# The last product of a short convolution: stepping on the output instead of on the inputs

## The chip, the cores and the metric

The kernel runs on one core of one Trainium2 chip. The metric is the device time of one execution in microseconds; the times given are medians over several runs. A profile is one execution taken by the hardware profiler, and its span runs from the first to the last instruction of the core.

## The reference

The inputs are bf16. A layernorm of `A_q` over its 640 channels feeds two branches, and the output is `x + A + B`, of shape 1x2048x640:

```
xn = layernorm(A_q)                                  # 2048 positions x 640 channels
# branch A: a short convolution (4 taps), a product with v, a long convolution over the sequence
k_shift[t] = sum over m of k[t - m] * shift_k[:, m]  # m = 0..3
kv   = k_shift * v
y    = irfft(rfft(kv padded to 4096) * rfft(ssm_k padded to 4096))[:2048] + kv * ssm_D
A    = xn * y
# branch B: a gated unit
B    = (sigmoid(xn @ w_gate) * (xn @ w_up)) @ w_down # 640 -> 1728 -> 640
out  = A_q + A + B
```

## The kernel before

Both branches run interleaved on the same engines. TensorE (PE) does the matmuls of branch B (gate and up on line 770, down on line 786) and also the transforms of the long convolution, written as small matmuls in four stages (st1 line 508, st2 line 528, st3 lines 580 and 582, st4 line 612). VectorE (DVE) and ScalarE (ACT) share the rest: results leave PSUM through `ev` (lines 314, 315 and 317), sigmoids are on ACT (lines 724, 729 and 735), the gated products on DVE (lines 726, 732 and 737), and the additions of the down product to `acc` on DVE (line 798).

The order of all this work is fixed. Each step is recorded as an operation with its reads and writes, and the lists `ORDER` and `ON_DVE` give the order of emission and the engine of the steps that could go to either. The durations that are passed to `dve(...)` or `pe(...)` don't change what is emitted. Each engine executes its own queue in that order. The matmuls of gate and up write two PSUM buffers `g`; the convolution uses three buffers `c`.

The 640 channels of the convolution are split into two halves of 4 groups of 80 channels; the partitions hold the 4 groups times 32 blocks of the sequence (n1), and the 64 positions in a block (n2) lie along the free dimension. A half is worked in 5 sub-blocks of 16 channels, 2 (`b`) times 8 (`j`), so there are 10 sub-blocks (`idx` 0 to 9). For each one `rec_kv` computes the taps and the product with v on DVE, all over 64 x 2 x 8 = 1024 elements per partition:

- line 470 multiplies a shifted slice of `kt` with a tap into `ta` or `tb`, line 471 does so for the third tap into the tile `kvt`, and line 475 adds the parts into `ta`;
- line 488, the last, multiplies `ta` with the slice of `vt` and writes `kvt`.

The tile `ta` has the layout [n, b, j] with j innermost. The slice of `vt` takes 8 neighbouring channels j, then the second 8 at 40 channels' distance, and the next position n at 80 channels' distance. The result must lie in `kvt` as [j, b, n] with n innermost, since st1 (line 508) loads, for each j, 128 neighbouring elements (b, n) of `kvt` as its stationary operand. `by_j` (line 451) gives this view of the tile. `PRM["KT"]` holds all ten indices, so the branch `kt` is taken each time.

So one instruction on line 488 also changes the layout: in the kernel before it is walked in the order of its output, (j, b, n), which is one run of 1024 elements, and reads `ta` in steps of 16 elements and `vt` in steps of 80.

Other lines that the text names: line 448 adds the diagonal `Dt` to every 64th element of a tile of the long filter `ht`; line 548 copies halves of the spectra `S` between partitions by DMA, and lines 552 to 567 form the products of the spectra on DVE; line 401 copies a table; lines 620 and 621 apply the result of the convolution to `acc`. Weights `w` of branch B come by DMA on SP's queue (lines 368 to 378).

Of the kernel before, what the change touches and what calls it, by code (L numbers as in the profile page):

```python
# [16 lines left out]
ALU = mybir.AluOpType  # L17
# [202 lines left out]
def kernel(  # L220
# [14 lines left out]
    nc = tc.nc  # L235
# [54 lines left out]
    tl = plan.tiles  # L290
# [18 lines left out]
    def dve(n, rate, fn, **kw):  # L309
        plan.op({"DVE": ((1.042 * n / rate + 70) * 1e-3, fn)}, **kw)  # L310
# [140 lines left out]
    def by_j(t):  # L451
        return t.rearrange("p b n j -> p (b n j)").rearrange("p (j b n) -> p j b n", j=JS, b=2)

    def rec_kv(idx, pri):
        half, sub = divmod(idx, NSUB)
        kb, vb = f"kt{half}", f"vt{half}"
        j0 = sub * JS
        a, o = f"ka{idx}", f"kvt{idx}"
        kr = [(kb, "h")] + [(kb, g) for g in range(G)]
        vr_ = [(vb, g) for g in range(G)]  # L460

        def sl(t, r0):
            return t[:, r0:r0 + N2, :].rearrange("p n (b j) -> p n b j", b=2)[:, :, :, j0:j0 + JS]

        def sh(m):
            s = sT[:, m:m + 1, half * HALF:(half + 1) * HALF].rearrange("p o (b j) -> p o b j", b=2)
            return s[:, :, :, j0:j0 + JS].to_broadcast((P, N2, 2, JS))

        def mul(c, m, al):
            dve(1024, 2, lambda: nc.vector.tensor_tensor(tl[c][:], sl(tl[kb], 3 - m), sh(m), ALU.mult) if c != o else  # L470
                nc.vector.tensor_tensor(tl[c].rearrange("p b n j -> p n b j"), sl(tl[kb], 3 - m), sh(m), ALU.mult),
                r=(kr if m else kr[1:]) + [("s",)], w=[(c,)], alloc=[(c, al)] if al else (), pri=pri)

        def add(c):
            dve(1024, 2, lambda: nc.vector.tensor_tensor(tl[a][:], tl[a][:], tl[c][:] if c != o else  # L475
                                                         tl[c].rearrange("p b n j -> p n b j"), ALU.add),
                r=[(c,)], w=[(a,)], pri=pri)
        t1, t2 = f"kb{idx}_1", f"kb{idx}_2"
        mul(a, 0, "ta")
        mul(t1, 1, "tb")  # L480
        mul(o, 2, "kvt")
        add(t1)
        mul(t2, 3, "tb")
        add(o)
        add(t2)
        kt = idx in PRM["KT"]
        form = "p n b j -> p j b n" if kt else "p n b j -> p b n j"
        dve(1024, 1 if kt else 2, lambda: nc.vector.tensor_tensor(by_j(tl[o]) if kt else tl[o][:], tl[a].rearrange(form),  # L488
                                                                  sl(tl[vb], 0).rearrange(form), ALU.mult),
            r=[(a,)] + vr_, w=[(o,)], pri=pri)  # L490

    def rec_st1(idx, x, pri, first):
# [364 lines left out]
    def conv():  # L857
        for s in range(-1, NI):
            nx = s + 1
            if nx < NI:  # L860
                rec_st1(nx, 1, ct(nx - 1) if nx else -1.0, True)
            if nx == 0:
                rec_kv(0, 8.0)
            if nx + 1 < NI:
                if nx + 1 == NSUB:
                    load_kv(1, ct(nx) - 10, nb=ct(nx) - PRM["KV1"])
                    load_h(1, 0, ct(nx) - 10, nb=ct(nx) - 20)
                if nx + 1 == NSUB + 2:
                    load_h(1, 1, ct(nx) - 10, nb=ct(nx) - 20)
                rec_kv(nx + 1, ct(nx))  # L870
            if nx < NI:
                rec_st1(nx, 0, ct(nx - 0.4), False)
            if s >= 0:
                rec_st2(s, ct(s))
                rec_prod(s, ct(s + 0.3))
                rec_st3(s, ct(s + 0.5))
                if s == NSUB - 1:
                    rec_st4(0, ct(s + PRM["ST4"]), False)
        rec_st4(1, ct(NI - 0.2), False)
# [48 lines left out]
```

## Time and profile before

| what | value |
|---|---|
| median of 3 runs | 260.01 us (258.31 to 262.99) |
| profiled execution, its own time | 262.01 us |
| its span | 259.9 us |
| granted TensorE clock, mean over the span | 0.978 |
| busy: PE, DVE, ACT | 244.0, 201.2, 175.5 us |
| line 488 on DVE | 10 instructions, 2131 to 2155 ns, first at 64.3 us, last at 194.4 us |
| line 508 on PE reading kvt | 320 matmuls, first at 67.6 us, last at 203.8 us |

The profile names an instruction by its line, its engine, its operation, and the tiles written and read (`out<-in`). Of a group it gives the shape, the number, the busy time in us, the mean of one in ns, and behind the second bar the engine's idle time just before these instructions with what ended most of it. A wait line reads "who waited <- for whom: us in total, times, longest". "Issue" is time in which an engine waited for nothing that the profile shows.

### The profile page before, as it was taken

The page shows a single profiled execution, that of the slowest core. Times are in us where ns is not written, and L with a number is a line of the kernel's source. Part 1 is how long each engine was busy: PE and PEld are TensorE (multiplying, and loading weights), DVE is VectorE, ACT ScalarE, POOL GpSimd, SP SyncE. Part 2 cuts the span into 40 slices and gives each one's busy share as a digit, 9 for nine tenths or more (in the row PEclk, how much of TensorE's full clock was granted, in tenths as well). Part 3 has the DMA queues.
Part 4 walks back from the last instruction along what each step waited for, and adds up shares of the span by engine and source line. Part 5 has one row for each costly group of instructions (what it writes and reads, how often), then busy time and mean ns, then how long its engine had stood idle before and what let it go on. Part 6 is the DMA issues. An engine that isn't in the chain of part 4 may idle for free.

```text
span 259.9 us, 9463 instructions
## 1 busy us (share of the span) xinstructions
PE 244.0 (94%) x4231; PEld 146.1 (56%) x4231; DVE 201.2 (77%) x337; ACT 175.5 (68%) x259; POOL 0.7 (0%) x6
## 2 busy tenths in 40 slices
PE   8999979999999999999999997899999999998980
PEld 2854436764445467666554554577676554556750
DVE  4623524768999899999999999579999998895630
ACT  3623779767888899788998885663899785441100
POOL 1000000000000000000000000000000000000000
PEclk9999999999999999999999999599999999999996
DMA  6999999999995528999999739934126476002823
GB/s 175 310 277 207 205 314 130 152 139 188 229 248 128 143 75 235 150 140 128 157 182 283 192 66 318 188 101 117 23 62 177 99 236 184 1 5 55 188 73 95
DMA packets 91024, 41.44 MB, mean 159 GB/s; under 512 B 66656, under 2 KB 88104, under 8 KB 90664
## 3 DMA queue, kind: packets, MB, share of 16 engines
q1 hardware_dynamic: 90600, 40.44, 73.6%
q8 instruction: 33, 0.54, 0.9%
q10 hardware_dynamic: 384, 0.41, 0.5%
q14 instruction: 7, 0.06, 0.1%
HBM read 30.61 MB, written 5.24 MB: 138 GB/s over the span
## 4 chain that ended last, share of the span: by engine, by line
PE 64%; DMA 18%; DVE 5%; SPq 4%; issue 3%; ACT 3%; DVEq 0%; ACTq 0%
PE g L786 25%; PE g L770 25%; DMA acc<-in_A_q_dram 9%; PE c L528 6%; DMA w<-in_B_w_up_dram 5%; DMA vt<-in_A_v_dram 3%; PE c L612 3%; PE c L580 3%; PE c L508 2%; DMA P<-S 2%; ACT S L314 1%; SPq L378 1%; SPq L352 1%; DVE hT L737 1%; SPq L827 1%
## 5 line engine op out<-in xcount | busy, mean ns | idle before, releaser
L770 PE MATMUL g<-xnT,w 128*128 128x512 bf16 x380 | 90.9, 379 | 2.6 <-ACT sig L735 1.3
L786 PE MATMUL g<-wd,hT 128*128 128x320 bf16 x448 | 68.5, 306 | 2.0 <-issue 2.0
L770 PEld LDWEIGHTS <-w 128*128 128x128 bf16 x380 | 34.7, 98 | 41.1 <-issue 2.6
L786 PEld LDWEIGHTS <-hT 128*128 128x128 bf16 x448 | 42.6, 99 | 19.4 <-issue 2.3
L314 ACT CAST S<-c 128x1024 bf16<-128x1024 f32 x40 | 39.4, 1026 | 8.1 <-PE c L528 8.0
L737 DVE TENSOR_TENSOR hT<-sig,g 128x512 bf16<-128x512 bf16 x32 | 21.9, 686 | 18.6 <-PE g L770 18.3
L770 PE MATMUL g<-xnT,V 128*128 128x512 bf16 x140 | 32.8, 379 | 0.0
L735 ACT ACTIVATE sig<-g 128x512 bf16<-128x512 f32 x32 | 19.2, 601 | 15.1 <-PE g L770 13.5
L798 DVE TENSOR_TENSOR acc<-g,acc 128x320 bf16<-128x320 f32 x32 | 15.5, 488 | 17.4 <-PE g L786 17.2
L528 PEld LDWEIGHTS <-Mt 64*128 64x128 f16 x1280 | 20.2, 96 | 8.7 <-issue 8.1
L528 PE MATMUL c<-T,Mt 64*128 64x64 bf16 x1280 | 22.8, 191 | 2.2 <-issue 2.2
L317 ACT ACTIVATE T<-c 128x1024 bf16<-128x1024 f32 x20 | 19.9, 1029 | 5.5 <-PE c L508 5.4
L770 PEld LDWEIGHTS <-V 128*128 128x128 bf16 x140 | 13.3, 98 | 15.7 <-DMA V<-in_B_w_up_dram 0.5
L488 DVE TENSOR_TENSOR kvt<-ta,vt 128x1024 bf16<-128x1024 bf16 x10 | 21.4, 2143 | 0.1
L314 ACT CAST V<-c 128x1024 bf16<-128x1024 f32 x18 | 18.2, 1026 | 3.2 <-PE c L580 3.1
L314 ACT CAST T<-c 128x1024 bf16<-128x1024 f32 x19 | 18.8, 1024 | 1.6 <-PE c L508 1.4
L729 ACT ACTIVATE sig<-g 128x512 bf16<-128x512 f32 x18 | 10.8, 602 | 5.0 <-PE g L770 3.3
L561 DVE TENSOR_TENSOR S<-S 128x1024 bf16<-128x1024 bf16 x20 | 13.8, 688 | 0.3
L475 DVE TENSOR_TENSOR ta<-ta,tb 128x1024 bf16<-128x1024 bf16 x20 | 13.8, 688 | 0.3
L470 DVE TENSOR_TENSOR tb<-kt,sT 128x1024 bf16<-128x1024 bf16 x20 | 13.8, 690 | 0.1
L567 DVE TENSOR_TENSOR S<-P 64x1024 bf16<-64x1024 bf16 x18 | 12.4, 689 | 0.6
L565 DVE TENSOR_TENSOR S<-S 64x1024 bf16<-64x1024 bf16 x18 | 12.4, 687 | 0.6
(82 smaller groups left out, 240.9 us busy)
## 6 DMA issues: line engine op xcount, KB each, us to landing
w<-in_B_w_gate_dram SPq DMA_DIRECT2D x7, 640.0 KB, 6.9
w<-in_B_w_up_dram SPq DMA_DIRECT2D x7, 640.0 KB, 5.2
P<-S SPq DMA_DIRECT2D x14, 256.0 KB, 3.7
kt<-in_A_k_dram SPq DMA_DIRECT2D x8, 320.0 KB, 6.3
vt<-in_A_v_dram SPq DMA_DIRECT2D x8, 320.0 KB, 7.1
xnd<-xq SPq DMA_DIRECT2D x4, 640.0 KB, 5.0
ht<-in_A_ssm_k_dram SPq DMA_DIRECT2D x16, 96.0 KB, 5.8
wd<-in_B_w_down_dram SPq DMA_DIRECT2D x3, 480.0 KB, 9.8
```

The lines of the kernel that those rows point to most:

```text
L314: fa = lambda: nc.scalar.copy(out=out_fn(), in_=in_fn())
L317: fa = lambda: nc.scalar.activation(out_fn(), in_fn(), ACT.Copy, scale=scale)
L470: dve(1024, 2, lambda: nc.vector.tensor_tensor(tl[c][:], sl(tl[kb], 3 - m), sh(m), ALU.mult) if c != o else nc.vector.tensor_tensor(tl[c]. ...
L475: dve(1024, 2, lambda: nc.vector.tensor_tensor(tl[a][:], tl[a][:], tl[c][:] if c != o else tl[c].rearrange("p b n j -> p n b j"), ALU.add) ...
L488: dve(1024, 1 if kt else 2, lambda: nc.vector.tensor_tensor(by_j(tl[o]) if kt else tl[o][:], tl[a].rearrange(form), sl(tl[vb], 0).rearrang ...
L528: nc.tensor.matmul(tl[c][:, b, 64 * kk:64 * kk + 64], lhsT=Mb[rows, k, 64 - 64 * r:192 - 64 * r], rhs=tl[T][rows, 2 * k + r].rearrange("p ...
L561: dve(n, 2, lambda b=b: nc.vector.tensor_tensor(X(b), X(b), H(b), ALU.mult), r=[(Z, b, 0)] + sr, w=[(S_, "p", b)], pri=pri + 0.01)
L735: act(512, lambda: nc.scalar.activation(tl[sg][:], pv(0), ACT.Sigmoid), r=[pk(0)], w=[(sg,)], alloc=[(sg, "sig")], pri=pri - 2000)
L737: dve(512, 1, lambda: nc.vector.tensor_tensor(hT[:, fc, :], tl[sg][:], pv(1), ALU.mult), r=[pk(1), (sg,)], w=[(hk, fc)], pri=pri - 2000)
L770: nc.tensor.matmul(tl[c][:], lhsT=w()[:, k, o:o + P], rhs=tl[X][:, k, :], start=(k == 0), stop=(k == NC - 1))
L786: nc.tensor.matmul(tl[pd[i]][:, 0:320], lhsT=hT[:, fc, t4 * P:(t4 + 1) * P], rhs=wd[:, fc, 320 * i:320 * i + 320], start=(fc == 0), stop=( ...
L798: dve(320, 1, lambda i=i, m=m, pd=pd: nc.vector.tensor_tensor(acc[:, m, 320 * i:320 * i + 320], tl[pd[i]][:, 0:320], acc[:, m, 320 * i:320 ...
```

## The change

Line 488 is walked in another order. The inputs are now taken as they lie, (n, b, j): `ta` as one run of 1024 elements, `vt` in runs of 8. The output tile is addressed through the same view `by_j`, with its dimensions permuted to (n, b, j), so that the same bytes get the same values: j moves by 128 elements in `kvt`, b by 64, n by 1. The branch for indices outside `PRM["KT"]` is rewritten in the same way and isn't taken. The file becomes one line shorter, so all lines from 488 on are one less in profiles of the changed kernel; the instruction itself stands under line 488 in the profile of the kernel before and under line 487 in that of the changed one.

```diff
         kt = idx in PRM["KT"]
-        form = "p n b j -> p j b n" if kt else "p n b j -> p b n j"
-        dve(1024, 1 if kt else 2, lambda: nc.vector.tensor_tensor(by_j(tl[o]) if kt else tl[o][:], tl[a].rearrange(form),
-                                                                  sl(tl[vb], 0).rearrange(form), ALU.mult),
+        dve(1024, 1 if kt else 2, lambda: nc.vector.tensor_tensor(
+            by_j(tl[o]).rearrange("p j b n -> p n b j") if kt else tl[o].rearrange("p b n j -> p n b j"), tl[a][:], sl(tl[vb], 0), ALU.mult),
             r=[(a,)] + vr_, w=[(o,)], pri=pri)
```

## The prediction

> **What bounds the kernel now.** I read the page's busy table and its 40 slices first, then the groups of instructions on VectorE with shapes kept apart, then busy time by stage, then the waits inside the stretch of the long convolution, and the timeline around the ten instructions that change.
>
> The busy table and the slices of the span (one digit is a fortieth, 6.5 us):
>
> ```profile
> PE 244.0 (94%) x4231; PEld 146.1 (56%) x4231; DVE 201.2 (77%) x337; ACT 175.5 (68%) x259; POOL 0.7 (0%) x6
> ...
> PE   8999979999999999999999997899999999998980
> ...
> DVE  4623524768999899999999999579999998895630
> ```
>
> The 77% of DVE is an average over unlike stages: from the tenth slice to the thirty-third its digit is 9 in most places, and so is that of PE. Two engines are nearly full at once there, so busy time by stage is needed (columns: stage, its length, busy us of PE, PEld, DVE, ACT and POOL with counts, granted clock, DMA share, GB/s):
>
> ```profile
> 57.00:160.00 103.00, 101.75 (x1867) 58.60 (x1866) 99.84 (x160) 90.55 (x123) 0.00 (x0) 1.00 0.86 174
> 160.00:175.00 15.00, 12.62 (x293) 8.29 (x293) 10.09 (x15) 8.23 (x10) 0.00 (x0) 0.77 0.77 180
> 175.00:215.00 40.00, 39.89 (x963) 25.34 (x961) 38.97 (x58) 31.04 (x38) 0.00 (x0) 1.00 0.45 116
> 215.00:252.00 37.00, 35.14 (x715) 22.29 (x713) 25.06 (x38) 11.78 (x18) 0.00 (x0) 1.00 0.36 88
> ```
>
> From 57 us to 252 us PE is idle for 1.25 + 2.38 + 0.11 + 1.86 = 5.6 us in all. That is the most that any faster DVE could give back. DVE is idle for 3.2 us of the first 103, for 4.9 us in a stretch where the granted clock is 0.77, and for 1.0 us of the 40 after it. So a DVE that gets slower has little room either. The waits of PE from 57 us to 252 us:
>
> ```profile
> PE c L528 <- issue: 2.2, 2, 1.9
> PE g L786 <- issue: 2.0, 2, 1.3
> PE g L770 <- DMA w<-in_B_w_up_dram: 1.0, 2, 0.5
> PE g L770 <- DVE hT L737: 0.2, 1, 0.2
> ```
>
> Only 0.2 us of it is put down to DVE. PE sets the time now, with DVE close behind it. The groups on VectorE that give the prices:
>
> ```profile
> L737 DVE TENSOR_TENSOR hT<-sig,g 128x512 bf16<-128x512 bf16 x32 | 21.9, 686 | 18.6 <-PE g L770 18.3
> L488 DVE TENSOR_TENSOR kvt<-ta,vt 128x1024 bf16<-128x1024 bf16 x10 | 21.4, 2143 | 0.1
> ...
> L475 DVE TENSOR_TENSOR ta<-ta,tb 128x1024 bf16<-128x1024 bf16 x20 | 13.8, 688 | 0.3
> ...
> L732 DVE TENSOR_TENSOR hT<-sig,hT 128x512 bf16<-128x512 bf16 x18 | 7.4, 421 | 1.5 <-ACT hT L314 1.1 <-ACT sig L729 0.3
> ...
> L315 DVE CAST V<-c 128x1024 bf16<-128x1024 f32 x2 | 2.4, 1218 | 0.0
> ...
> L448 DVE TENSOR_TENSOR ht<-ht,Dt 128x48 bf16<-128x48 bf16 x2 | 0.7, 372 | 0.0
> ...
> L448 DVE TENSOR_TENSOR ht<-ht,Dt 128x32 bf16<-128x32 bf16 x2 | 0.6, 294 | 0.0
> ```
>
> L488 is the changed line: 2143 ns each, ten times, the dearest 1024-element instruction on this engine. The reader should see how far it lies above 1218 ns (1024 elements one at a time) and 688 ns (1024 bf16 elements in dense order).
>
> **The change, part by part.** Nothing is added, removed or moved: the changed kernel's instruction list has the same instructions in the same order on every engine, with the same DMAs. Only the access patterns of ten instructions differ; the output of each is now a pattern of 64x2x8 elements instead of one run of 1024. The bytes of kvt are the same, so L508, which reads it on PE, costs what it did.
>
> *The fixed part.* L732 (512 elements) takes 421 ns and L475 (1024) takes 688, so 512 dense elements cost 267 ns and the fixed part is 421 - 267 = 154 ns. At one element at a time, L737 (686 for 512) and the cast of V (1218 for 1024) give (1218 - 686) / 512 = 1.04 ns per element, and 1024 of them cost 154 + 1065 = 1219 ns.
>
> *What is removed.* L488 takes 2143 - 1219 = 924 ns more than that, 0.90 ns per element. Its output is one run; ta is read in steps of 16 elements (32 bytes) and vt in steps of 80 (160 bytes). So 0.90 ns is what the two stepped reads cost, and it goes: ta becomes one run of 1024, vt runs of 8 elements (runs of 8 cost nothing visible as the output of L471 or of the cast of V).
>
> *What is added.* The output goes out in steps of 128 elements (256 bytes), eight times, then 128 bytes on from the start, then one element on: every element lands away from the one before. The trace has one row that writes single bf16 elements this way: L448 adds Dt into every 64th element of ht (128 bytes), reading ht in that step too. From 32 to 48 elements it goes from 294 to 372 ns, 4.9 ns per element; over the 48, (372 - 154) / 48 = 4.5 ns. Against 1.04 that is 3.5 to 3.8 ns extra, for three stepped streams together, on the same bytes for the read and the write. How much belongs to the write is not shown. Bounds: none of it (1219 ns, a gain of 0.92 us each, 9.2 us on ten), or all of it (1219 + 1024 x 3.8 = 5.1 us, a loss of 3.0 us each, 30 us). A price as for a dense output, 688 ns and 14.5 us gained, is a still lower end; L448, with a stepped output, lies so far above it that I give it little, and PE's 5.6 us cap the gain in either case. Between these ends I go by the row that the new write is nearest to, L448, and give half of its 3.5 ns to the write, 1.75 ns: 1219 + 1792 = 3.01 us, 0.87 us more than now. The sum on DVE is 10 x 0.87 = +8.7 us.
>
> The Trainium skill, page "Vector Engine (DVE) Microarchitecture Reference", section "5.2 Measured stream behaviour on trn2 (trn3 not measured)", speaks against a gain in another way: for 4-byte elements it has an output that hops on every element at 1.71 to 2.51 ns per column, the same as two sources that both do (1.73 to 2.51). The 1.94 ns that L488 shows now, (2143 - 154) / 1024, lies inside its span for the sources; no row here shows its span for an output alone. An estimate by that page is 1.9 to 2.7 us for the new instruction and -2.4 to +5.8 us on the ten.
>
> *What lies on the path.* Behind the ten on DVE are queued the products of the gated part (L737, L732), which free the two g buffers that PE's L770 writes, and the steps of the next kvt and the products of the spectra (L552 to L567). When L488 is 0.87 us late, L737 is late, then a g buffer, then PE. The ten start at 64.3, 71.3, 82.2, 96.9, 116.5, 137.1, 145.3 and 163.6 us, one between there and 194, and at 194.4. L508 reads kvt 1.1 us after the first and second end, 0.2 us after the sixth, and 3 to 11 us after the others up to the eighth, so mostly the engine's queue hands the delay on and not kvt itself.
>
> Cover: the seven before 160 us add 6.1 us; DVE's idle time from 64 to 160 us is 96 - 93.5 = 2.5 us, which hides at most that, and 3.6 us remain. The eighth is free: 3.9 us of idle time stand behind it (DVE waits there for L786 on PE), in a stretch of reduced clock; without that stretch it costs 0.9. The last two add 1.7 us against 1.1 of idle time, 0.6 remains. So the end moves by 4.2 us if every idle gap can be used, and by 8.7 if none can. Gaps of a few tenths sit where DVE already waits for PE, which is then late as well, and PE has nothing to catch up with; I take the middle, 6.5 us. DMAs lose no price of their own: the swaps (L548) start when S is written, and shift with the rest.
>
> *Against what.* The profiled execution took 262.0 us, with a span of 259.9; its sum is 268.5 us with a span of 266.4. It lies 2 us above the median of the runs, 260.0, and the stretch of reduced clock explains that (2.4 us of PE idle time in it). Against the median the forecast is 266.5 us.
>
> **The rivals.**
>
> 1. *The write costs what the reads cost.* At 0.90 ns per element for stepped output the ten stay at 2.14 us; between 1.8 and 2.5 us each the sum on DVE is -3.4 to +3.6 us, and PE's cap and DVE's idle time leave 258 to 263, about 260.5. For it: the 0.90 is a measured price of stepping on this engine. Against it: it is a price for reads, and the row with a stepped write is at four times as much.
> 2. *The write is free, and the kernel gets faster.* The place is L488 alone, the price 1.2 to 1.8 us, the gain on DVE 3.4 to 9.2 us. It decides from the point at which PE waits for DVE: 0.2 us are shown for certain, 5.6 us is the cap. With 2.5 us through earlier g buffers the time is 257.5; only at the cap does it pass 2%, at 254.4. For it: two stepped streams become one. Against it: L448, and how little PE waits for DVE.
> 3. *The write takes nearly all of L448's price.* From 3.7 to 5.1 us each the sum is +16 to +30 us. Idle time hides some 4 of it, then nothing more, and DVE becomes the engine that sets the end: 272 to 286, about 277. With the reads of L448 priced as in L488 (0.90), its write would be at 2.6 to 2.9 ns and L488 at 3.9 to 4.2 us, so this is not far off. Against it: L448 reads and writes the same bytes, in larger steps than L488 reads, and has only 48 elements.
> 4. *The change does nothing*, because the loop order is put back when the kernel is built: 260. The list of instructions shows the new output pattern, so hardly.
>
> **How the numbers follow.** Forecast (2.5 to 3.7 us each, 262 to 272): 0.48. Rival 1: 0.24. Rival 3: 0.15. Rival 2: 0.11. Rival 4: 0.02. A measurement of this kernel can tell about 2% from no change, here 254.8 and 265.2. Slower by more: rival 3 and 0.41 of the forecast's 0.48, 0.56. Faster by more: under half of rival 2, 0.05. Within 2%: 0.39. The range runs from rival 2's middle, 257, to the middle of rival 3, 279: about 0.05 is left below and 0.11 above. The forecast alone spans 262 to 272.
>
> **What would show it.** In the profile after, the group of this line on VectorE (one line earlier) should stand at 2.5 to 3.7 us; L448 and L475 should keep their means. DVE's busy sum should rise by 8.7 us, its idle time between 64 and 160 us should shrink below 2.5 us, and PE's idle time between 57 and 252 us should grow from 5.6 to about 12 us, now put down to DVE (hT, kvt) rather than to issue. The forecast is wrong if the group stands at or below 2.14 us, which decides for rival 1 or 2, or above 3.7. The step from DVE to the end is wrong if the group rises as said and PE's idle time doesn't.

## The result, and the profile after

The changed kernel takes 282.4 us (median of 4 runs, 281.9 to 283.5) against 259.9 us for the kernel before: 1.089 times as long, 95% interval 1.083 to 1.096. Ratios and their intervals leave out runs of over 1.5% above the fastest of the same kernel (of the kernel before one of four here, 263.0 us), so they differ a little from the quotients of the medians. The time lies outside the range of 257 to 279 us, on the side of the third rival. The profiled execution took 281.9 us, with a span of 279.8.

The busy table and the slices of the kernel after:

```profile
PE 244.3 (87%) x4231; PEld 145.8 (52%) x4231; DVE 225.3 (81%) x337; ACT 176.5 (63%) x259; POOL 0.7 (0%) x6
...
PE   8999999996889697996996969599796999798980
...
DVE  4515327699999989999999999999999998785720
```

PE does the same work, 244 us, but many of its digits from the tenth slice on are 5 to 8 where nearly all were 9; those of DVE are 9 nearly throughout. DVE is now the fuller of the two, and on the chain of work that ended last (part 4 of the page) its share of the span goes from 5% to 33%, that of PE from 64% to 46%. The groups on VectorE of the kernel after:

```profile
L487 DVE TENSOR_TENSOR kvt<-ta,vt 128x1024 bf16<-128x1024 bf16 x10 | 46.4, 4638 | 0.1
...
L475 DVE TENSOR_TENSOR ta<-ta,tb 128x1024 bf16<-128x1024 bf16 x20 | 13.7, 687 | 0.3
...
L448 DVE TENSOR_TENSOR ht<-ht,Dt 128x48 bf16<-128x48 bf16 x2 | 0.7, 372 | 0.0
```

The product went from 2143 to 4638 ns; its neighbours stand where they stood. What the queue loses by that is read from the timelines, here of the second product, of the kernel before and of the kernel after (start, length):

```profile
71.29 2.15 DVE L488 TENSOR_TENSOR kvt<-ta,vt 128x1024 bf16<-128x1024 bf16 x1
73.35 0.76 DVE L732 TENSOR_TENSOR hT<-sig,hT 128x512 bf16<-128x512 bf16 x2
```

```profile
72.40 4.63 DVE L487 TENSOR_TENSOR kvt<-ta,vt 128x1024 bf16<-128x1024 bf16 x1
76.65 0.96 DVE L731 TENSOR_TENSOR hT<-sig,hT 128x512 bf16<-128x512 bf16 x2
```

The next instruction starts 2.06 us after the product before and 4.25 us after it now, 0.4 us ahead of the product's recorded end. But it takes longer itself: the pair on the second line ends 73.35 + 0.76 - 71.29 = 2.82 us after the product's start before and 76.65 + 0.96 - 72.40 = 5.21 us after it now. To the end of the instruction behind it, each product costs the queue 2.4 to 2.5 us more, 24 us on the ten, where the means say 24.9 and DVE's busy sum grows by 24.1. By the ratio the end moves by 23.2 us, with an interval of 21.6 to 24.8 (by the medians, 22.5). The stages of the kernel after (PE, PEld, DVE, ACT, POOL busy as in the prediction's table):

```profile
57.00:160.00 103.00, 89.37 (x1478) 50.79 (x1477) 99.24 (x136) 77.76 (x104) 0.00 (x0) 0.98 0.78 156
...
57.00:272.00 215.00, 188.69 (x3826) 113.55 (x3824) 196.68 (x266) 141.26 (x184) 0.00 (x0) 0.99 0.60 132
```

From 57 us to the end of the matmuls, now at 272 us, PE is idle for 215 - 188.7 = 26.3 us; it was 5.6. DVE's idle time in the first of these stages is 3.8 us against 3.2 before, and from 64 us to 160 us it is 96 - 92.9 = 3.1 us against 2.5: it did not shrink. The waits of PE in the kernel after:

```profile
PE g L769 <- DVE hT L736: 5.8, 4, 2.4
PE c L507 <- DVE kvt L487: 4.9, 3, 2.2
PE g L769 <- DVE acc L797: 4.8, 3, 2.4
PE g L785 <- DVE acc L797: 4.0, 4, 1.8
```

19.5 us are put down to DVE, where it was 0.2: 14.6 of them to work queued behind a product (hT, acc) and 4.9 to kvt itself.

### The profile page after: what moved, and what is told of

It is laid out like the page before. It is cut to its first block, busy times and chain, and to the rows that moved or that the text cites. A ratio compares the mean times of both kernels' runs of the same rounds, so it can differ in the third digit from the quotient of the medians.

```text
span 279.8 us, 9463 instructions
## 1 busy us (share of the span) xinstructions
PE 244.3 (87%) x4231; PEld 145.8 (52%) x4231; DVE 225.3 (81%) x337; ACT 176.5 (63%) x259; POOL 0.7 (0%) x6
## 4 chain that ended last, share of the span: by engine, by line
PE 46%; DVE 33%; issue 6%; ACT 6%; DMA 5%; ACTq 0%; SPq 0%; DVEq 0%
PE g L769 24%; PE g L785 14%; DVE kvt L487 12%; DMA w<-in_B_w_up_dram 4%; DVE ta L475 3%; PE c L611 3%; DVE P L557 2%; DVE tb L470 2%; PE c L527 2%; DVE acc L797 2%; DVE S L560 2%; DVE S L566 2%; DVE hT L736 2%; DVE S L564 1%; ACT S L314 1%
## 5 line engine op out<-in xcount | busy, mean ns | idle before, releaser
L785 PE MATMUL g<-wd,hT 128*128 128x320 bf16 x448 | 66.3, 299 | 6.3 <-DVE acc L797 4.0
L487 DVE TENSOR_TENSOR kvt<-ta,vt 128x1024 bf16<-128x1024 bf16 x10 | 46.4, 4638 | 0.1
L769 PE MATMUL g<-xnT,V 128*128 128x512 bf16 x140 | 34.3, 392 | 3.5 <-DVE hT L736 3.5
L797 DVE TENSOR_TENSOR acc<-g,acc 128x320 bf16<-128x320 f32 x32 | 16.6, 522 | 12.8 <-PE g L785 12.5
L527 PE MATMUL c<-T,Mt 64*128 64x64 bf16 x1280 | 22.5, 190 | 2.0 <-issue 2.0
L728 ACT ACTIVATE sig<-g 128x512 bf16<-128x512 f32 x18 | 10.8, 600 | 10.9 <-PE g L769 7.9
```

Of the source, the lines that this page charges most:

```text
L527: nc.tensor.matmul(tl[c][:, b, 64 * kk:64 * kk + 64], lhsT=Mb[rows, k, 64 - 64 * r:192 - 64 * r], rhs=tl[T][rows, 2 * k + r].rearrange("p ...
L769: nc.tensor.matmul(tl[c][:], lhsT=w()[:, k, o:o + P], rhs=tl[X][:, k, :], start=(k == 0), stop=(k == NC - 1))
L785: nc.tensor.matmul(tl[pd[i]][:, 0:320], lhsT=hT[:, fc, t4 * P:(t4 + 1) * P], rhs=wd[:, fc, 320 * i:320 * i + 320], start=(fc == 0), stop=( ...
L797: dve(320, 1, lambda i=i, m=m, pd=pd: nc.vector.tensor_tensor(acc[:, m, 320 * i:320 * i + 320], tl[pd[i]][:, 0:320], acc[:, m, 320 * i:320 ...
```

## The experiments

### What a stepped write costs by itself

Two things were open: whether the price comes from the write alone, and from which property of it. The kernel before got a row of single instructions on dead data behind all its work. The functions `out`, `src`, `runs` and `rd` make the access patterns; the comment names what is not dense.

```diff
     plan.emit(plan.table(), make)
+    nc.vector.tensor_tensor(O_[:, 0:1024], A_[:, 0:1024], B_[:, 0:1024], ALU.mult)      # L915 dense
+    nc.vector.tensor_tensor(out(2, 512), src(A_, 512), src(B_, 512), ALU.mult)          # L916 write step 2 elements
...                                                                                      # L917 to L930: 4, 8, 16 ... 1024
+    nc.vector.tensor_tensor(out(128, 8), src(A_, 8), src(B_, 8), ALU.mult)              # L922 write step 128
+    nc.vector.tensor_tensor(out(136), src(A_), src(B_), ALU.mult)                       # L924 write step 136
...                                                                                      # L931 the pattern of the kernel after
+    nc.vector.tensor_tensor(runs(128, 2), srun(A_, 2), srun(B_, 2), ALU.mult)           # L932 write runs of 2, L933 runs of 4
...                                                                                      # L937 4-byte elements, step 64
...                                                                                      # L939 the pattern of the kernel before
+    nc.vector.tensor_tensor(dn(O_), rd(A_, 16), dn(B_), ALU.mult)                       # L940 one input read in steps of 16
...                                                                                      # L945 both inputs in steps of 128
...                                                                                      # L946 160 elements, write step 64; L947 in place
+    nc.vector.tensor_copy(out(128), src(A_))                                            # L948 copy, write step 128
...                                                                                      # L951 ScalarE copy, write step 128
```

> The kernel before, with a row of single VectorE instructions (and three on ScalarE) behind all its work, each 1024 bf16 products of dense inputs unless said, so that the disputed price is measured alone. Theory A (each lone 2-byte element that is written costs about 3.3 ns more than a dense one, whatever the step): every write step of 16 to 1024 elements takes about 4.6 us, steps of 130, 136, 144 no less than 128; runs of 2 and 4 take clearly less; 4-byte elements written in a step take clearly less than 4.6 us. Theory B (the price comes from steps of 256 bytes or other powers of two that fall on one bank): steps 128, 256, 512, 1024 take about 4.6 us, but 130, 136, 144 and 160 under 3 us. Theory C (any hop costs, on reads as on writes): one stepped read of 128 elements takes 4 us or more as well, and 4-byte elements take as long as 2-byte ones. The pattern of the kernel after should show 4.6 us and that of the kernel before 2.14 us in every case.

The groups of that run behind the kernel's work (one instruction each):

```profile
L951 ACT COPY V<-acc 128x1024 bf16<-128x1024 bf16 x1 | 4.7, 4732 | 0.0
...
L922 DVE TENSOR_TENSOR V<-acc,wd 128x1024 bf16<-128x1024 bf16 x1 | 4.7, 4709 | 0.0
...
L924 DVE TENSOR_TENSOR V<-acc,wd 128x1024 bf16<-128x1024 bf16 x1 | 4.6, 4648 | 0.0
...
L931 DVE TENSOR_TENSOR V<-acc,wd 128x1024 bf16<-128x1024 bf16 x1 | 4.6, 4576 | 0.0
...
L945 DVE TENSOR_TENSOR V<-acc,wd 128x1024 bf16<-128x1024 bf16 x1 | 2.4, 2441 | 0.0
L948 DVE COPY V<-acc 128x1024 bf16<-128x1024 bf16 x1 | 2.4, 2439 | 0.0
...
L939 DVE TENSOR_TENSOR V<-acc,wd 128x1024 bf16<-128x1024 bf16 x1 | 2.1, 2148 | 0.0
...
L940 DVE TENSOR_TENSOR V<-acc,wd 128x1024 bf16<-128x1024 bf16 x1 | 2.0, 1991 | 0.0
...
L937 DVE TENSOR_TENSOR V<-acc 128x1024 f32<-128x1024 f32 x1 | 1.9, 1894 | 0.0
...
L916 DVE TENSOR_TENSOR V<-acc,wd 128x1024 bf16<-128x1024 bf16 x1 | 1.3, 1296 | 0.0
...
L932 DVE TENSOR_TENSOR V<-acc,wd 128x1024 bf16<-128x1024 bf16 x1 | 1.0, 1033 | 0.0
L947 DVE TENSOR_TENSOR V<-V,wd 128x160 bf16<-128x160 bf16 x1 | 0.9, 894 | 0.0
L946 DVE TENSOR_TENSOR V<-acc,wd 128x160 bf16<-128x160 bf16 x1 | 0.9, 872 | 0.0
L933 DVE TENSOR_TENSOR V<-acc,wd 128x1024 bf16<-128x1024 bf16 x1 | 0.7, 694 | 0.0
```

The patterns of before and after stand at 2148 and 4576 ns alone, so nothing around them makes the price. Step 136 costs what step 128 costs, and so do 160 and 512 (4601 and 4699, not shown): theory B, of one bank, falls. One input in steps of 128 takes 1873 or 1882 ns (not shown), both take 2441, and 4-byte elements that are written in steps 1894: theory C falls. Theory A held for every step that it named, 16 to 1024 elements (4442 to 4717 ns), but not "whatever the step": at 2 elements the price is nearly gone. Five readings matter here:

- In a product, a lone bf16 element costs (4709 - 154) / 1024 = 4.4 ns where it is written, a lone 4-byte element (1894 - 154) / 1024 = 1.7 ns.
- A copy on VectorE with the same lone bf16 writes (L948) takes 2439 ns, 2.2 ns per element. So the 4.4 is the price of a product of two inputs and not of every instruction.
- In the pattern of the kernel before, one stepped input costs nearly what two do: 1991 ns with `ta` alone stepped, 2149 with `vt` alone (not shown), 2148 with both. That doesn't hold for every step: with 128 elements it is 1873 to 1882 for one and 2441 for both.
- L946 has dense inputs and the step of L448: (872 - 154) / 160 = 4.5 ns per element, as L448 has. Reading the same bytes in place (L947) adds 22 ns. The whole price of L448 is its write.
- In runs of 4 elements the write costs as if dense, 694 ns, and in runs of 2 only half as much again.

The Trainium skill, "Vector Engine (DVE) Microarchitecture Reference", section "5.2 Measured stream behaviour on trn2 (trn3 not measured)", has 1.71 ns for a 4-byte output that hops on every element by 4 KiB; the 1.7 ns here agrees, at 256 bytes. The section measures streams of 4-byte elements; those that cost 4.4 ns here are of 2 bytes.

A second row asked what exactly makes an element dear.

```diff
     plan.emit(plan.table(), make)
...                                                                                      # L916 lone, starting on element 1; L917 runs of 2 from element 0
+    nc.vector.tensor_tensor(O_[:, 1:1025].rearrange('p (j x) -> p j x', j=8)[:, :, 0:128].rearrange('p j (y r) -> p y j r', r=2), srun(A_, 2), srun(B_, 2), ALU.mult)  # runs of 2, start 1
...                                                                                      # the line above is L918; runs of 4 from element 0 (L919), 1 (L920), 2 (L921)
...                                                                                      # 512 lone elements, step 2 (L922), 4 (L924), 6 (L926), 8 (L927), 12 (L928)
...                                                                                      # L930: 512 lone 4-byte elements, step 4
...                                                                                      # L932: bf16 in, lone 4-byte out; L934: 4-byte in, lone bf16 out
```

> The kernel before, with a second row of single VectorE products behind all its work, on what exactly makes a written element dear. Theory A1 (what costs is an aligned 4-byte word written in part): runs of 2 that start on an odd element fill no word and should cost about as much as two lone elements, 4 us or more, against 1.03 us when they start on an even one; runs of 4 from an odd start should cost clearly more than 0.69 us, from start 2 not. Theory A2 (what costs is a lone element, wherever it lies): runs of 2 cost about 1.03 us and runs of 4 0.69 us at every start. Width of the output or of the input: bf16 inputs with lone 4-byte results should take about 1.9 us and 4-byte inputs with lone bf16 results about 4.7 us, if the output's width decides. 512 lone bf16 elements at steps of 2 to 12 elements should go from about 0.7 us (step 2, as the first row's 1.30 us for 1024) to about 2.4 us (step 8), with step 4 near 1.3; lone 4-byte results at the steps 2 to 8 stay under 1.2 us.

```profile
L917 DVE TENSOR_TENSOR V<-acc,wd 128x1024 bf16<-128x1024 bf16 x1 | 1.0, 1028 | 0.0
L918 DVE TENSOR_TENSOR V<-acc,wd 128x1024 bf16<-128x1024 bf16 x1 | 3.0, 3012 | 0.0
...
L920 DVE TENSOR_TENSOR V<-acc,wd 128x1024 bf16<-128x1024 bf16 x1 | 1.9, 1879 | 0.0
L921 DVE TENSOR_TENSOR V<-acc,wd 128x1024 bf16<-128x1024 bf16 x1 | 0.8, 814 | 0.0
...
L922 DVE TENSOR_TENSOR V<-acc,wd 128x512 bf16<-128x512 bf16 x1 | 0.7, 728 | 0.0
...
L924 DVE TENSOR_TENSOR V<-acc,wd 128x512 bf16<-128x512 bf16 x1 | 1.3, 1291 | 0.0
...
L927 DVE TENSOR_TENSOR V<-acc,wd 128x512 bf16<-128x512 bf16 x1 | 2.4, 2423 | 0.0
L928 DVE TENSOR_TENSOR V<-acc,wd 128x512 bf16<-128x512 bf16 x1 | 2.4, 2401 | 0.0
...
L932 DVE TENSOR_TENSOR V<-acc,wd 128x1024 f32<-128x1024 bf16 x1 | 1.9, 1891 | 0.0
...
L934 DVE TENSOR_TENSOR V<-acc 128x1024 bf16<-128x1024 f32 x1 | 4.7, 4711 | 0.0
```

The output's width decides: 1891 ns for lone 4-byte results of bf16 inputs, 4711 for lone bf16 results of 4-byte inputs. A pair on an even element costs 1028 ns, on an odd one 3012: not neighbours as such make a write cheap, but an aligned 4-byte word written whole. Runs of 4 take 692 ns from element 0 (not shown), 1879 from element 1 and 814 from element 2. A2 falls, and A1 had the direction right and the size too high (4 us or more). Lone elements cost 0.55 ns per element of the step, from 728 ns at step 2 through 1291 at 4 to 2423 at 8, 16 bytes, and no more beyond (2401 at 12).

The rows of these products fit one count, an estimate made after the runs and not tested by another. Each time the write moves on to another aligned 16-byte piece of the tile, it costs some 4.4 ns if it writes a 4-byte word there in part, and some 1.7 ns if it writes whole words only, and the whole never takes less than a dense output does. The 512 elements at step 2 lie in 128 pieces: 128 x 4.4 + 154 = 717 ns (728 measured). Runs of 2 from element 1 touch 640 pieces, since every fourth run lies in two: 2970 ns (3012). Runs of 4 touch 384 pieces from element 1, 1844 ns (1879), and also from element 2, there with whole words only, 384 x 1.7 + 154 = 807 ns (814). What in the memory does this was not measured.

### How lost time on VectorE reaches the end

Three kernels have the product as before and added work on dead data at that place. In the first it stands behind the product, in the second ahead of it, in the third it is smaller.

```diff
+            nc.vector.tensor_tensor(by_j(tl[o]), ta_, vt_, ALU.mult)        # the product, as before
+            nc.vector.tensor_tensor(by_j(tl[a]), vt_, vt_, ALU.mult)        # dead, the same pattern
+            nc.vector.tensor_tensor(flat, flat, flat, ALU.mult)             # dead, 720 elements
```

> The kernel before with two more VectorE instructions right behind each of the ten products with v: a copy of the product's pattern on dead data (2.05 us from start to start) and a dense product of 720 elements (some 0.45 us), 2.5 us in all, as much as the changed product is longer. kvt itself is on time. Theory Q (only the time that VectorE's queue loses matters): the kernel takes 278 to 285 us, as the kernel after. Theory K (the lateness of kvt itself, waited for by the first transform, makes a good part of the loss): at least 5 us less than the kernel after, 270 to 277 us. Theory W (the stepped write disturbs other engines' accesses beside its own length): clearly less than after here and in the next run too.

```diff
+            nc.vector.tensor_tensor(flat, flat, flat, ALU.mult)             # 720 elements
+            nc.vector.tensor_tensor(by_j(tl[o]), vt_, vt_, ALU.mult)        # overwritten by the next
+            nc.vector.tensor_tensor(by_j(tl[o]), ta_, vt_, ALU.mult)        # the product, as before
```

> The same two added instructions ahead of each of the ten products, so that kvt is late by 2.5 us too. Theory Q: equal to the run with the two behind, within 2 us, 278 to 285 us. Theory K: 280 to 285 us here, 5 us or more above the run with the two behind. Theory W: both clearly under 280 us.

They take 285.5 and 286.5 us (ratios 1.102, interval 1.092 to 1.111, and 1.109, 1.098 to 1.120), against 260.4 us for the kernel before, measured beside them. The waits of PE, first with the work behind:

```profile
PE g L775 <- DVE hT L742: 6.2, 3, 2.7
PE g L775 <- ACT sig L740: 4.8, 2, 2.5
PE g L775 <- DVE acc L803: 4.6, 3, 2.1
PE g L791 <- DVE acc L803: 4.4, 3, 2.1
```

and with the work ahead:

```profile
PE c L513 <- DVE kvt L494: 5.5, 3, 2.5
PE g L775 <- DVE hT L742: 5.4, 4, 2.5
```

The row "c <- kvt" is there when kvt is late and gone when it is on time, and the end hardly differs. So kvt's lateness shows in the waits but does not set the loss; where PE doesn't wait for it, it waits for hT, sig or acc instead. Theory K falls. Both kernels lie a little above what Q expected, since the added work was larger than I had sized it: in their timelines the instruction after the group starts 4.8 us after its start, 2.75 more than before, not 2.5. (Each of the two instructions behind the first starts 0.03 to 0.04 us after the recorded end of the one ahead of it, whose tile it reads or writes; behind the product in the kernel before, the next mostly starts some 0.1 us ahead of that end.) Theory W falls as well: with no stepped write at all, the loss is as large.

```diff
+            nc.vector.tensor_tensor(by_j(tl[o]), ta_, vt_, ALU.mult)        # the product, as before
+            nc.vector.tensor_tensor(flat, flat, flat, ALU.mult)             # dead, 1024 elements
+            nc.vector.tensor_tensor(flat[:, 0:360], flat[:, 0:360], flat[:, 0:360], ALU.mult)
```

> The kernel before with 0.86 us more on VectorE behind each of the ten products (two dense products on dead data, 1024 and 360 elements), which is the loss that the prediction had sized, 8.6 us in all. If VectorE's idle time hides at most the 2.5 us that it has between 64 and 160 us, the kernel takes 6 to 8 us more than before, 266 to 268 us; if short gaps hide all of it while it is small, 260 to 263; if each delay grows on its way, over 270.

It takes 269.0 us against 259.4, ratio 1.038 (1.032 to 1.043). By start-to-start distance the group takes 3.18 us, 1.12 more than before, 11.2 us on the ten instead of the 8.6 intended. By the ratios, the end moves by 9.8 us of these 11.2 (interval 8.4 to 11.2), by 23.2 of the 24 in the kernel after, and by 26.3 and 28.2 of the 27.5 in the two larger runs. So lost time arrives almost one for one at every size; about 1.4 us may be hidden in the smallest dose, but the intervals, some 1.4 us to either side there and more in the others, don't tell that from nothing.

### What dense writes bring

If runs of 4 bytes and more are cheap, the product can be written in runs of 2, 4 or 8 channels, with its inputs read in runs of 8, and TensorE loads its stationary operand with a step. The first two against the kernel after:

```diff
+    def by_r(t):
+        return t.rearrange("p b n j -> p (b n j)").rearrange("p (j b n r) -> p j b n r", j=JS // RUN, b=2, r=RUN)
...
+        dve(1024, 2, lambda: nc.vector.tensor_tensor(
+            by_r(tl[o]).rearrange("p j b n r -> p b n j r"), tl[a].rearrange("p n b (j r) -> p b n j r", r=RUN),
+            sl(tl[vb], 0).rearrange("p n b (j r) -> p b n j r", r=RUN), ALU.mult),
...
-                    st = (tl[hb][rows, hj + j, :, :] if x else by_j(tl[f"kvt{idx}"])[rows, j] if idx in PRM["KT"]
+                    st = (tl[hb][rows, hj + j, :, :] if x else by_r(tl[f"kvt{idx}"])[rows, j // RUN, :, :, j % RUN] if idx in PRM["KT"]
```

> The product is written in runs of 2 channels at a step of 256 elements, and read in the same runs: kvt has the layout [j/2, b, n, 2], and TensorE loads its stationary operand in steps of 4 bytes. Theory A (a lone 2-byte element is what costs; a 4-byte pair costs 0.66 ns more than a dense one): the product takes about 1.03 us as in the table of single instructions, 1.1 us less than before, though the step of the output is twice that of the kernel after. Theory D (what costs is the long step of the output, on any run): 3 us or more. At the end, TensorE's idle time of 5.6 us caps the gain: 255 to 260 us if the stationary loads in steps of 4 bytes cost nothing; up to 3 us worse if they do.

> The same with runs of 4 (8 bytes), layout [j/4, b, n, 4], stationary operand in steps of 8 bytes. Theory A: 0.69 us for the product, 1.45 us less than before each, 14.5 us of VectorE in all; the end gains no more than in the run with pairs by more than 1 us, since TensorE sets it: 254 to 260 us. Theory D: 2 us or more for the product.

The version with runs of 8 needs no new layout; `KT` is empty, so that `kvt` stays in [b, n, j]:

```diff
-                ZC=(1, 2, 3, 4, 5, 6, 7, 8, 9), KT=(0, 1, 2, 3, 4, 5, 6, 7, 8, 9), TD=1)
+                ZC=(1, 2, 3, 4, 5, 6, 7, 8, 9), KT=(), TD=1)
```

> The same with runs of 8, kvt in [b, n, j] as it is when no index takes the transposing branch: the product's output is dense, and the stationary operand is loaded in steps of 16 bytes. 0.69 us for the product in every theory. If stepped loads of the stationary operand cost TensorE something, it shows here first: the 320 loads from kvt then take longer than 93 ns and the kernel 261 to 266 us; if not, 254 to 260 us as with runs of 4.

The product in the groups with runs of 2, of 4 and of 8, in that order:

```profile
L493 DVE TENSOR_TENSOR kvt<-ta,vt 128x1024 bf16<-128x1024 bf16 x10 | 10.6, 1061 | 0.1
```

```profile
L493 DVE TENSOR_TENSOR kvt<-ta,vt 128x1024 bf16<-128x1024 bf16 x10 | 6.9, 688 | 0.1
```

```profile
L488 DVE TENSOR_TENSOR kvt<-ta,vt 128x1024 bf16<-128x1024 bf16 x10 | 6.9, 687 | 0.1
```

Runs of 2 step twice as far as the kernel after (512 bytes) and take 1061 ns: theory D falls, theory A holds inside the kernel too. The times are 259.9, 258.9 and 263.5 us; the ratios to before are 1.003 (1.000 to 1.006), 0.999 (0.995 to 1.002) and 1.018 (1.013 to 1.023). So 10.8 and 14.6 us less on VectorE by the means (9.8 and 13.2 by its busy sum) bring nothing that can be measured, as the 0.2 us that PE waited for DVE said. With runs of 8 the loads of the stationary operand step by 16 bytes and show it, as that run's expectation had it. The kernel before, then the one with runs of 8:

```profile
L508 PE MATMUL c<-Ft,kvt 32*128 32x64 f16 x320 | 4.1, 189 | 0.0
...
L508 PEld LDWEIGHTS <-kvt 32*128 32x128 bf16 x320 | 2.9, 93 | 3.4 <-issue 2.1 <-DVE ta L470 0.4 <-DVE hT L732 0.4
```

```profile
L508 PE MATMUL c<-Ft,kvt 32*128 32x64 f16 x320 | 6.9, 224 | 0.0
...
L508 PEld LDWEIGHTS <-kvt 32*128 32x128 bf16 x320 | 5.8, 160 | 3.4 <-issue 2.1 <-DVE ta L470 0.8 <-DVE hT L737 0.4
```

Before, a load took 93 ns and the busy sums were 2.9 us (loads) and 4.1 us (matmuls); now they are 160 ns, 5.8 and 6.9 us. The 2.8 us more of matmuls can account for a part of the 4.1 us by which the median moves; that they reach the end is argued and not shown, and where the rest goes was not followed. With steps of 4 bytes a load still takes 93 ns, with 8 bytes 113. No version beat the kernel before; those with runs of 2 and 4 equal it within 0.6%, with a VectorE that has 10 to 15 us less to do.

## Why the prediction was wrong

**What bounds the kernel: right.** PE sets the time before, with DVE close behind. Taking time from DVE brings nothing (runs of 2 and 4), adding time moves the end nearly one for one (three runs with dead work). The cap of 5.6 us on any gain was not tested at its edge, but no version came near it.

**The fixed part: right. The price of the reads: right as a sum.** By the two rows of single instructions, 1024 and 512 lone elements at step 8 take 4689 and 2423 ns, which leaves 157 ns for the fixed part against the 154 of the prediction. The 0.90 ns for the reads was worked out from the 2143 ns themselves, so that the pattern takes 2148 ns alone confirms only that nothing around it makes the price. It was named as what the two stepped reads cost, and one of them alone (`vt`, 2149 ns) costs it all. And the "none of it" of 1219 ns is no floor: pairs of channels with dense inputs take 1033.

**The step that failed is the half.** The prediction read 3.5 to 3.8 ns extra off L448, said that how much of it belongs to the write is not shown, and gave "half of its 3.5 ns to the write, 1.75 ns". By its own formula the kernel after shows (4638 - 1219) / 1024 = 3.34 ns, and L946 against L947 shows that in L448 too the write is all of it: 872 of 894 ns. The new product was sized at 3.01 us and measured at 4.64; the bound of 5.1 us held. With 4.64 in its place, and the same 2.2 us hidden, the prediction's own sum gives 260.0 + 25.0 - 2.2 = 282.8 us, and 282.4 were measured: the size of this one term is what was off. The stated reasons for a smaller share, that L448 reads and writes the same bytes and reads in larger steps, were worth 22 ns in 160 elements. Subtracting the 0.90 of the reads, as the third rival did (3.9 to 4.2 us), was wrong for the same reason: the prices of reads and writes are not added here. With a lone write at 4.5 ns per element it hardly shows whether an input steps (L947 against L946), and L448, where both do, is at 4.5 too.

**The estimate by the page, 1.9 to 2.7 us,** missed by more, for it holds for 4-byte elements. (A slip there: in section 5.2 of that page of the Trainium skill, 1.73 ns is for one source that hops; for two it has 1.75 to 2.51. The estimate uses the figures for the output and stands.)

**The path to the end: right in size, not in how.** The prediction let 2.2 of 8.7 us disappear in DVE's idle time; the run with a like dose shows 1.4 of 11.2, with 0 and 2.8 both inside its interval. That the sizes agree is partly luck: DVE's idle time between 64 and 160 us "should shrink below 2.5 us" and did not (3.1 us in the kernel after). When DVE is late, PE is late, and DVE's waits for PE move along with it. The third rival let some 4 us be hidden and put the centre at 277, 5 us short, mostly by its price: with 4.64 us for the product and the same 4 us hidden, its sum is 281.

**Signs:** DVE's busy sum rose by 24.1 us and not 8.7. PE's idle time grew, as it should, but to 26.3 us and not 12; and its waits turned from issue to DVE (hT, acc, kvt), as said.

**The chances:** slower had 0.56, but the case that came true, with 3.7 to 5.1 us for the product, had only 0.15. The one row of the trace with such a write pointed straight at it.

## What to carry to other kernels

When a layout of 2-byte elements has to change on the way through VectorE, let the reads step and the writes run: in products of two inputs on this chip a lone bf16 write at 16 bytes or more from the last cost 4.4 ns per element (in a copy 2.2), two inputs stepped as in the kernel before 1.9, and an output in aligned runs of 4 or 8 bytes 0.9 or 0.5 ns per element with dense inputs, all beside a fixed 154 ns. If the trace has one row like the new instruction, take its price whole, or measure it by itself, before sharing it out among causes. With two nearly full engines in fixed queues, as here, time taken from the second brought nothing, while time added to it arrived almost one for one. And what an instruction costs its queue is read up to the end of the one behind it: the mean duration alone, or the distance to the next start alone, misses an overlap.

## What was not expected of the hardware

- The price of a lone bf16 write grows with the distance to the next, up to 16 bytes: 728, 1291 and 2423 ns for 512 elements at 4, 8 and 16 bytes. A step of 4 bytes costs little over element by element (1296 ns for 1024 against 1219), if twice what a dense output does (681).
- A ScalarE copy with a write step of 128 elements took 4732 ns, as long as the product on VectorE; a VectorE copy took 2439.
- The instruction behind a stepped write started 0.4 us before that write's recorded end, and took 0.2 us longer than elsewhere.
- Loads of the stationary operand took nothing more at a step of 4 bytes (93 ns), 20 ns more at 8 bytes and 67 ns at 16.
